# A diagonal block's score tiles computed over part of their columns, the rest read back transposed

## The chip, the cores and the metric

The program runs on one core of one Trainium2 chip. The metric is the device time of one execution in microseconds (us), the median of several runs. Beside the runs there is one profiled execution, whose trace gives every duration below. Engine names are the profile's: PE is TensorE's matmul, PEld its weight load, DVE is VectorE, ACT ScalarE, POOL GpSimd, SP SyncE, which issues the DMAs spoken of here.

## What is computed

Three layers follow each other. The change touches the first alone.

```python
def _attn_ref(u, v, z):              # u, v: 8 x 3072 x 256; z: 8 x 3072 x 64
    scores = (1.0 / S) * np.matmul(z, z.transpose(0, 2, 1))
    attn = np.maximum(scores, 0.0) ** 2
    return u * np.matmul(attn, v)
# x = that, as 24576 rows of 256
# _moe_ref:  h = x @ w_in (256 x 2048);  x = (h * sigmoid(h)) @ w_out
# _moe2_ref: each row goes to the one expert of 8 with the largest logit,
#            gate * sigmoid(...) * (relu(row @ w1[e]) @ w2[e])
```

The scores of a batch are a symmetric matrix: `attn[k, q] == attn[q, k]`.

## The kernel before, in words

All matmuls are in fp32r, in a split form: an operand is stored as a rounded part `hi` and a rest `lo`, and a product takes three passes (hi by hi, lo by hi, hi by lo). Each batch has six blocks of 512 query columns (`q`, `NS` = 4 tiles of 128 each), 48 blocks over the eight batches, written (batch, q) below. A block goes over 24 key tiles of 128 rows (`k`). One key tile is one attention item:

- Its front (lines 257 to 281) makes the 128 x 512 tile `a` of squared scores. Two score passes on PE (lines 269 and 270), Relu and Square on ACT (272 and 273), a copy to `hi` on ACT or DVE (275, 277). One step later DVE takes the rest, `lo = a - hi` (251).
- Its back, three steps (`LOOK`) later, adds the tile to the block's output with six passes of 512 columns (lines 293 to 295).

Because scores are symmetric, a tile whose key block lies below the query block (`mirrored`, from block (0, 3) on) isn't computed. When block `k // NS` computed the transposed tile, `keep` (line 239) stored it to DRAM in a buffer `sym`; `load_sym` (line 225) fetches it in four DMAs that put each 32 x 32 piece in its place, and `flip` (line 232) transposes the pieces on DVE. Such an item has no score passes, one ACT copy (264) and two DVE operations.

The order of the keys in a block is `key_order`: first the four tiles of the next query block, then all others from 0 upwards. So the block's own four tiles, those on the diagonal, stand next to each other, and all four are computed in full.

Between the attention items stand the items of the first MoE layer for the block before. The order is written out by hand (`order`): two MoE items, three attention items, and again, eight times a block. A MoE item has six passes of 512 columns in its front (324), a Sigmoid on ACT (326), a product on DVE (328), `hi` on ACT (331), `lo` on DVE (333), and twelve passes of 256 columns in its back (358 to 360).

Everything else is a task with a release and a due step, taken from a queue: a task that isn't due is run early only when a credit allows it. An item gives credit when its back is done: a MoE item 1.1, a computed attention item 0.8, a mirrored one nothing (`spare`). Most of these tasks are the router's dot products on DVE (line 368), 32 for each block, two to a task of 0.72.

The loads of `z`, `v` and mirrored tiles go through one stream in order of their due steps. Each takes one of four `raw` buffers. A load is put on SP when its turn comes in the stream and its `since` step is past; the loads behind it in the stream wait for it. The operation that uses a load is emitted at its due step, or before if credit allows.

Of the kernel before, what the change touches and what calls it, by code (L numbers as in the profile page):

```python
# [9 lines left out]
F32 = mybir.dt.float32  # L10
# [3 lines left out]
AF = mybir.ActivationFunctionType  # L14
# [3 lines left out]
P = 128  # L18
TQ = 512
NS = TQ // P  # L20
# [3 lines left out]
SQ = 32  # L24
# [9 lines left out]
def r32(ap):  # L34
    return ap.bitcast(F32)
# [7 lines left out]
def moe_chain(tc, zT, uT, vp, win, wout, w12, wgT, wogT, out):  # L43
    nc = tc.nc
    B, NQ, DZ, _ = zT.shape
# [4 lines left out]
    KT = S // P  # L50
# [17 lines left out]
    with ExitStack() as ctx:  # L68
        ec = ctx.enter_context
        dram = ec(tc.tile_pool(name="dram", bufs=1, space=bass.MemoryType.DRAM))  # L70
        cp = ec(tc.tile_pool(name="cp", bufs=1))
# [10 lines left out]
        def mk(pool, shape, dt, tag, bufs):  # L82
            uid[0] += 1
            return pool.tile(shape, dt, tag=tag, name=f"{tag}_{uid[0]}", bufs=bufs)

        def psum():
            return mk(pp, [P, TQ], F32, "ps", 4)

        def accum():
            return mk(pp, [P, 2, TQ], F32, "acc", 2)  # L90
# [58 lines left out]
        def later(steps, cost, fn, slack=2):  # L149
            i = now[0] + steps  # L150
            bisect.insort(queue, (i + slack, i, len(tasks), cost, fn))
            tasks.append(None)
# [32 lines left out]
        def load_u(b, q):  # L185
            t = mk(cp, [P, ND, TQ], F32, "xf", 1)
            x = xs[(b, q)] = [t[:, c, :] for c in range(ND)]
            for c in range(ND):
                nc.sync.dma_start(out=x[c], in_=uT[b, q, :, c, :])
# [19 lines left out]
        def mirrored(b, q, k):  # L209
            return k // NS < q and (b, q) >= (0, 3)  # L210

        def key_order(b, q):
            if not any(mirrored(b, q, k) for k in range(KT)):
                return list(range(KT))
            lead = list(range((q + 1) * NS, (q + 2) * NS)) if q < NQ - 1 else list(range(q * NS, KT))
            return lead + [k for k in range(KT) if k not in lead]

        sym, flipped = {}, {}

        def load_sym(b, q, k):  # L220
            def f(t):
                src = sym[b, k // NS, q]
                for g in range(P // SQ):
                    o = k % NS * P + g * SQ
                    nc.sync.dma_start(out=t[g * SQ:(g + 1) * SQ].rearrange("t (j d) -> t j d", d=SQ),
                                      in_=src[:, o:o + SQ].rearrange("(j t) d -> t j d", t=SQ))
            return f

        def flip(b, q, k):
            def f(t):  # L230
                a = flipped[b, q, k] = mk(cp, [P, TQ], F32, "t1", 4)
                nc.vector.transpose(a, t)  # L232
            return f

        def keep(b, q, k, a):
            key = (b, q, k // NS)
            if key not in sym:
                sym[key] = dram.tile([TQ, TQ], F32, name=f"sym_{b}_{q}_{k // NS}")
            nc.sync.dma_start(out=sym[key][k % NS * P:(k % NS + 1) * P, :], in_=a)

        def att_items(b, q, hold):
            st = {}
            early = (b, q) < (0, 2)
            ks = key_order(b, q)

            def front(i):
                k = ks[i]

                def low(a, hi, lo):
                    def f():  # L250
                        nc.vector.tensor_tensor(out=lo, in0=a, in1=r32(hi), op=ALU.subtract)  # L251
                        if k // NS > q and mirrored(b, k // NS, q * NS):
                            keep(b, q, k, a)
                    return f

                def f():
                    if i == KT - UAT:
                        load_u(b, q)
                    hi = mk(cp, [P, TQ], F32R, "hi", 4)
                    lo = mk(cp, [P, TQ], F32R, "lo", 4)  # L260
                    st[i] = (hi, lo)
                    if mirrored(b, q, k):
                        a = flipped.pop((b, q, k))
                        nc.scalar.activation(hi, a, AF.Copy)  # L264
                        return low(a, hi, lo)
                    h, l = qs[(b, q)]
                    ps = psum()
                    lhs = hl[k // NS][:, (k % NS) * P:(k % NS + 1) * P]
                    nc.tensor.matmul(ps, lhs, h, start=True, stop=False)  # L269
                    nc.tensor.matmul(ps, lhs, l, start=False, stop=True)  # L270
                    a = mk(cp, [P, TQ], F32, "t1", 4)
                    nc.scalar.activation(a, ps, AF.Relu)
                    nc.scalar.activation(a, a, AF.Square)
                    if (early and q and k % 2) or (not early and (q or k % 3)):
                        nc.scalar.activation(hi, a, AF.Copy)  # L275
                    else:
                        nc.vector.tensor_copy(hi, a)
                    return low(a, hi, lo)
                return f

            def back(i):
                k = ks[i]

                def f():
                    hi, lo = st.pop(i)
                    if i == 0:
                        st["acc"] = accum()
                    acc = st["acc"]
                    for c in range(ND):
                        o = k % 2 * D + c * P  # L290
                        h = vh[k // 2][:, o:o + P]
                        l = vl[k // 2][:, o:o + P]
                        nc.tensor.matmul(acc[:, c, :], h, hi, start=i == 0, stop=False)  # L293
                        nc.tensor.matmul(acc[:, c, :], h, lo, start=False, stop=False)  # L294
                        nc.tensor.matmul(acc[:, c, :], l, hi, start=False, stop=i == KT - 1)  # L295
                    if i == KT - 1:
                        later(1, 1.2, finish, 0)
                        later(3, 1.2, lambda: split_x(b, q, hold == "last"), 0)
                return f

            def finish():
                for c, x in enumerate(xs[(b, q)]):
                    nc.vector.scalar_tensor_tensor(out=x, in0=st["acc"][:, c, :], scalar=AS, in1=x, op0=ALU.mult, op1=ALU.mult)

            def spare(k):
                return EARLY if early else 0.0 if mirrored(b, q, k) else 0.8

            return [Item(front(i), back(i), spare(k)) for i, k in enumerate(ks)]
# [399 lines left out]
        for n in range(3, NBLK):  # L708
            for g in range(8):
                if n > 3 or g >= 2:  # L710
                    j = (g - 2) % 8 * GM
# [16 lines left out]
        def att_step(n, k):  # L728
            return at_["a", n, k]
# [12 lines left out]
        def prep(due, rel, load, use, since=0):  # L742
            stream.append((due, rel, len(stream), load, use, since))
# [5 lines left out]
        def last_use(n, keys):  # L749
            direct = [k for k in keys if not mirrored(*blocks[n], k)]  # L750
            return used(n, direct) if direct else 0
# [12 lines left out]
        for n, (b, q) in enumerate(blocks):  # L764
            if q == 0:
                for j in range(NHL):
                    if n:
                        due = att_step(n - 2, KT // 2 + 2 * j) if j < NQ - 2 else att_step(n - 1, KT // 2) if j < NQ - 1 else att_step(n, KT // 2)
                        rel = max(last_use(n - t, range(j * NS, (j + 1) * NS)) for t in range(1, NQ + 1)) + 1
                    else:  # L770
                        due, rel = max(att_step(n, j * NS) - 2, 0), 0
                    prep(due, rel, load_zz(b, j), f_hl(j))
            prep(att_step(n, 0) - (5 if n else 0), att_step(n - 1, KT // 2) if n else 0, load_zz(b, q), f_hh((b, q)))
            for i, k in enumerate(key_order(b, q)):
                if mirrored(b, q, k):
                    o = key_order(b, k // NS)
                    since = max(att_step(n - q + k // NS, o.index(q * NS + s)) for s in range(NS)) + 2
                    prep(att_step(n, i), att_step(n, i), load_sym(b, q, k), flip(b, q, k), since)
            if q == 0:
                for j in range(KT // 2):  # L780
                    rel = used(n - 1, (2 * j, 2 * j + 1)) + LOOK + 1 if n else 0
                    due = att_step(n, 2 * j) + (-1 if n else 1)
                    prep(due, rel, load_flat(vp[b, :, 2 * j:2 * j + 2, :].rearrange("p a d -> p (a d)")), f_split(vh[j], vl[j], b, due))
        stream.sort()
        staged = []
# [84 lines left out]
        for n in range(NBLK):  # L870
            rel = moe_end[n] + LOOK + 2
            due = moe_end[n + 1] if n + 1 < NBLK else max(m2_at[min(NA // 4, 8)], rel)
# [138 lines left out]
```

## Time and profile before

| | us |
|---|---|
| median of 3 runs (lowest and highest) | 5292.82 (5292.71 to 5293.24) |
| the profiled execution | 5293.77 |
| its span, first to last instruction | 5292.0 |
| PE busy | 5189.7 (98%) |
| PE weight load busy | 4529.6 (86%) |
| DVE busy | 3897.6 (74%) |
| ACT busy | 3234.9 (61%) |

A mean of 98% for PE is over stages that differ: blocks (0, 0) to (0, 2), a stage in which attention and MoE items alternate (277.8 to about 4069 us), and the experts. The granted clock is 0.995 of full speed over the span and 1.00 in the middle stage. A matmul's printed duration includes the way through the array, which overlaps the next pass; what a pass costs in a row of passes is the distance between two starts.

### The profile page before, as it was taken

How to read it: one execution, taken by the hardware profiler on the slowest of the kernel's cores; microseconds unless marked ns; L12 is line 12 of the kernel's file. 1: busy time of each engine (PE TensorE's matmuls, PEld its weight loads, DVE VectorE, ACT ScalarE, POOL GpSimd, SP SyncE). 2: the span in 40 equal slices, each digit the busy share in tenths (PEclk: the TensorE clock that was granted, in tenths of full speed). 3: DMA queues.
4: the chain of work that ended last, by engine and by line, in shares of the span. 5: the costliest groups of instructions: out<-in, count | busy, mean ns of one | idle time of the engine just before them, and what ended most of it. 6: DMA issues, size and time to landing. Idle time of an engine off the chain costs nothing.

```text
span 5292.0 us, 88328 instructions
## 1 busy us (share of the span) xinstructions
PE 5189.7 (98%) x30026; PEld 4529.6 (86%) x30026; DVE 3897.6 (74%) x9627; ACT 3234.9 (61%) x5804; POOL 491.2 (9%) x503
## 2 busy tenths in 40 slices
PE   7999999999999999999999999999999899999998
PEld 5888888888888888888888888888888799999998
DVE  8778767866786778677767877687677786666687
ACT  6655665666566666665666566656654455555576
POOL 3100000000000000000000000000000121111111
PEclk9999999999999999999999999999999899999999
DMA  5134324433442334234333432343333456555564
GB/s 155 57 81 86 102 80 92 93 89 77 86 104 85 81 77 110 81 77 84 108 80 82 87 106 75 83 91 95 86 83 80 133 171 201 175 175 175 178 229 157
DMA packets 1334523, 574.63 MB, mean 109 GB/s; under 512 B 1173421, under 2 KB 1206830, under 8 KB 1318192
## 3 DMA queue, kind: packets, MB, share of 16 engines
q1 hardware_dynamic: 1315248, 517.00, 38.1%
q0 software_dynamic: 18816, 51.93, 2.7%
q8 instruction: 237, 3.88, 0.3%
q14 instruction: 222, 1.82, 0.1%
HBM read 393.54 MB, written 178.42 MB: 108 GB/s over the span
## 4 chain that ended last, share of the span: by engine, by line
PE 84%; DVE 8%; ACT 3%; issue 2%; DMA 2%; SPq 0%; POOL 0%; DVEq 0%; ACTq 0%; POOLq 0%
PE ps L324 17%; PE ps L663 10%; PE acc L360 9%; PE acc L358 9%; PE acc L359 9%; PE acc L295 8%; PE acc L294 8%; PE acc L293 8%; PE ps L269 3%; PE ps L270 3%; DVE lo L251 1%; DMA raw<-sym 1%; DVE lo L333 1%; DVE junk L368 1%; DVE t L328 1%
## 5 line engine op out<-in xcount | busy, mean ns | idle before, releaser
L328 DVE TENSOR_TENSOR t<-ps,t 128x512 f32<-128x512 f32 x768 | 529.4, 689 | 655.5 <-ACT t L326 649.8
L359 PE MATMUL acc<-woutl,hi 128*128 128x256 f32 x3600 | 998.3, 277 | 0.0
L331 ACT ACTIVATE hi<-t 128x512 fp32r<-128x512 f32 x768 | 486.0, 633 | 764.1 <-DVE t L328 764.1
L294 PE MATMUL acc<-lo,vh 128*128 128x512 f32 x2304 | 911.1, 395 | 37.7 <-DVE lo L251 37.5
L295 PE MATMUL acc<-hi,vl 128*128 128x512 f32 x2304 | 910.9, 395 | 0.0
L293 PE MATMUL acc<-hi,vh 128*128 128x512 f32 x2304 | 903.3, 392 | 0.0
L360 PE MATMUL acc<-wouth,lo 128*128 128x256 f32 x3072 | 858.5, 279 | 42.5 <-DVE lo L333 42.4
L251 DVE TENSOR_TENSOR lo<-t,hi 128x512 fp32r<-128x512 f32 x1152 | 791.4, 688 | 130.9 <-ACT hi L275 128.9
L358 PE MATMUL acc<-wouth,hi 128*128 128x256 f32 x3072 | 853.9, 278 | 0.0
L359 PEld LDWEIGHTS acc<-woutl,hi 128*128 128x128 f32 x3600 | 678.0, 188 | 32.4
L368 DVE CUSTOM_DVE_ANT_0 junk<-rec,wg 128x256 f32<-128x256 f32 x1536 | 648.7, 422 | 35.3
L360 PEld LDWEIGHTS acc<-wouth,lo 128*128 128x128 f32 x3072 | 577.9, 188 | 53.0 <-DVE lo L333 50.9
L326 ACT ACTIVATE t<-ps 128x512 f32<-128x512 f32 x768 | 454.6, 592 | 265.5 <-PE ps L324 263.7
L358 PEld LDWEIGHTS acc<-wouth,hi 128*128 128x128 f32 x3072 | 577.6, 188 | 26.2
L294 PEld LDWEIGHTS acc<-lo,vh 128*128 128x128 f32 x2304 | 433.9, 188 | 158.3 <-DVE lo L251 56.5
L434 POOL DMA_INDIRECT scr<-rec,si x192 | 206.7, 1077 | 3767.2 <-DVE lo L251 1705.9
L264 ACT ACTIVATE hi<-t 128x512 fp32r<-128x512 f32 x468 | 295.8, 632 | 418.7 <-DVE t L232 333.9
L333 DVE TENSOR_TENSOR lo<-t,hi 128x512 fp32r<-128x512 f32 x768 | 523.6, 682 | 13.1 <-issue 0.2
L293 PEld LDWEIGHTS acc<-hi,vh 128*128 128x128 f32 x2304 | 434.2, 188 | 98.8
L295 PEld LDWEIGHTS acc<-hi,vl 128*128 128x128 f32 x2304 | 434.3, 189 | 91.4
L666 ACT ACTIVATE hi<-ps 128x512 fp32r<-128x512 f32 (+1 forms) x488 | 254.7, 522 | 396.9 <-PE ps L663 375.3
L668 DVE SCALAR_TENSOR_TENSOR lo<-ps,hi 128x512 fp32r<-128x512 f32 (+1 forms) x488 | 288.2, 591 | 245.8 <-ACT hi L666 244.0
(449 smaller groups left out, 10572.9 us busy)
## 6 DMA issues: line engine op xcount, KB each, us to landing
raw<-in_w_dram SPq DMA_DIRECT2D x122, 1024.0 KB
sym<-t SPq DMA_DIRECT2D x468, 256.0 KB
raw<-sym SPq DMA_DIRECT2D x1872, 64.0 KB
raw<-in_zT_dram SPq DMA_DIRECT2D x192, 128.0 KB
raw<-in_vp_dram SPq DMA_DIRECT2D x96, 256.0 KB
xf<-in_uT_dram SPq DMA_DIRECT2D x96, 256.0 KB
xg<-scr SPq DMA_DIRECT2D x39, 544.0 KB
x<-scr SPq DMA_DIRECT2D x304, 64.0 KB
```

Source lines behind the costliest of these rows:

```text
L251: nc.vector.tensor_tensor(out=lo, in0=a, in1=r32(hi), op=ALU.subtract)
L293: nc.tensor.matmul(acc[:, c, :], h, hi, start=i == 0, stop=False)
L294: nc.tensor.matmul(acc[:, c, :], h, lo, start=False, stop=False)
L295: nc.tensor.matmul(acc[:, c, :], l, hi, start=False, stop=i == KT - 1)
L324: nc.tensor.matmul(ps, win_at(w, c, f_), x[c], start=c == 0 and i == 0, stop=c == ND - 1 and i == 2)
L328: nc.vector.tensor_tensor(out=g, in0=ps, in1=sg, op=ALU.mult)
L333: return lambda: nc.vector.tensor_tensor(out=lo, in0=g, in1=r32(hi), op=ALU.subtract)
L358: nc.tensor.matmul(y[:, s, :], a, wh, start=first and s % per_bank == 0, stop=False, skip_group_check=True)
L359: nc.tensor.matmul(y[:, s, :], a, wl, start=False, stop=False, skip_group_check=True)
L360: nc.tensor.matmul(y[:, s, :], l, wh, start=False, stop=last, skip_group_check=True)
L368: nc.vector.tensor_tensor_reduce(out=j, in0=a, in1=w, scale=1.0, scalar=0.0, op0=ALU.mult, op1=ALU.add, accum_out=res)
L663: nc.tensor.matmul(ps[:, 0:T], w[:, o:o + P], y[c][:, 0:T], start=c == 0 and j == 0, stop=c == ND - 1 and j == 2)
```

## The change

From block (0, 3) on, a new function `columns(b, q, k)` says how many of a tile's 512 columns are fetched and not computed: all for a tile below the diagonal, none above it, and on the diagonal 0, 128, 256 and 384 for the block's own tiles 0 to 3 (called own tile 0 to 3 below).

- The two score passes, Relu and Square of an own tile go over the columns from `w` on. The columns before `w` are fetched from `sym` and transposed into the same buffer, by the same `load_sym` and `flip`, cut to `w` columns.
- Own tiles 0 to 2 are stored by `keep`, from the column behind the diagonal piece on (`c`).
- `key_order` spreads the own tiles: they are the block's items 0, 6, 12 and 18. Between them the tiles of the next block come first, then the others. For q = 0 it changes the order too.
- An own tile's `since` is two steps behind the last own tile before it, and `v`'s due steps follow the new order. `spare` isn't changed: an own tile still gives a credit of 0.8.

The core of the diff:

```diff
+        def columns(b, q, k):
+            if (b, q) < (0, 3):
+                return 0
+            return TQ if k // NS < q else k % NS * P if k // NS == q else 0
         def key_order(b, q):
-            if not any(mirrored(b, q, k) for k in range(KT)):
+            if not any(columns(b, q, k) for k in range(KT)):
                 return list(range(KT))
-            lead = list(range((q + 1) * NS, (q + 2) * NS)) if q < NQ - 1 else list(range(q * NS, KT))
-            return lead + [k for k in range(KT) if k not in lead]
+            own = range(q * NS, (q + 1) * NS)
+            lead = [k for k in range(KT) if k // NS == q + 1]
+            o = lead + [k for k in range(KT) if k not in lead and k not in own]
+            for s, k in enumerate(own):
+                o.insert(s * KT // NS, k)
+            return o
...
-                nc.vector.transpose(a, t)
+                w = columns(b, q, k)
+                nc.vector.transpose(a[:, 0:w], t[:, 0:w])
...
+            c = (k % NS + 1) * P if k // NS == q else 0
-            nc.sync.dma_start(out=sym[key][k % NS * P:(k % NS + 1) * P, :], in_=a)
+            nc.sync.dma_start(out=sym[key][k % NS * P:(k % NS + 1) * P, c:TQ], in_=a[:, c:TQ])
...
-                        if k // NS > q and mirrored(b, k // NS, q * NS):
+                        if k // NS > q and mirrored(b, k // NS, q * NS) or k // NS == q and k % NS < NS - 1 and columns(b, q, k + 1):
                             keep(b, q, k, a)
...
-                    nc.tensor.matmul(ps, lhs, h, start=True, stop=False)
-                    nc.tensor.matmul(ps, lhs, l, start=False, stop=True)
-                    a = mk(cp, [P, TQ], F32, "t1", 4)
-                    nc.scalar.activation(a, ps, AF.Relu)
-                    nc.scalar.activation(a, a, AF.Square)
+                    w = columns(b, q, k)
+                    nc.tensor.matmul(ps[:, w:TQ], lhs, h[:, w:TQ], start=True, stop=False)
+                    nc.tensor.matmul(ps[:, w:TQ], lhs, l[:, w:TQ], start=False, stop=True)
+                    a = flipped.pop((b, q, k)) if w else mk(cp, [P, TQ], F32, "t1", 4)
+                    nc.scalar.activation(a[:, w:TQ], ps[:, w:TQ], AF.Relu)
+                    nc.scalar.activation(a[:, w:TQ], a[:, w:TQ], AF.Square)
...
-                if mirrored(b, q, k):
+                if columns(b, q, k):
                     o = key_order(b, k // NS)
-                    since = max(att_step(n - q + k // NS, o.index(q * NS + s)) for s in range(NS)) + 2
+                    since = max(att_step(n - q + k // NS, o.index(q * NS + s)) for s in range(NS if mirrored(b, q, k) else k % NS)) + 2
                     prep(att_step(n, i), att_step(n, i), load_sym(b, q, k), flip(b, q, k), since)
...
-                    due = att_step(n, 2 * j) + (-1 if n else 1)
+                    due = min(att_step(n, key_order(b, q).index(2 * j + s)) for s in range(2)) + (-1 if n else 1)
```

Two places show how this moves instructions. The first is DVE in block (2, 3), from the end of items 6 to 8 to the next attention items. `t` from `ps` is a MoE item's product, `lo` a rest, `junk` with the row behind it one router dot product, STREAM_TRANSPOSE a flip. Before:

```order
L328 TENSOR_TENSOR t_3378_14656<-ps_14647,t_3377_14654 128x512
L251 TENSOR_TENSOR lo_14624<-t_3368_14616,hi_14623 128x512
L328 TENSOR_TENSOR t_3383_14677<-ps_14668,t_3382_14675 128x512
L333 TENSOR_TENSOR lo_14659<-t_3378_14656,hi_14658 128x512
L232 STREAM_TRANSPOSE t_3386_14689<-raw_14499 128x512
```

In the change, the same place:

```order
L342 TENSOR_TENSOR t_3415_14927<-ps_14918,t_3414_14925 128x512
L264 TENSOR_TENSOR lo_14895<-t_3405_14887,hi_14894 128x512
L382 ISA junk_14939,L_14878<-rec_14775,wg 128x256
L382 ISA L_14878 128x1
L382 ISA junk_14941,L_14878<-rec_14775,wg 128x256
L382 ISA L_14878 128x1
L342 TENSOR_TENSOR t_3422_14952<-ps_14943,t_3421_14950 128x512
L347 TENSOR_TENSOR lo_14930<-t_3415_14927,hi_14929 128x512
L244 STREAM_TRANSPOSE t_3425_14964<-raw_14828 128x512
```

Item 6 is own tile 1 here, and its credit of 0.8 lets one more pair of dot products run between the two MoE products. Earlier in the same piece item 6's flip is 128 columns wide, where it was 512.

The second place is SP in block (2, 0), around the first fetched piece of an own tile. `sym_2_0_0` holds the diagonal block of batch 2, `sym_2_0_1` and `sym_2_0_2` the blocks beside it. Before, the loads of `sym` in this block were those for the next block and came behind the store of tile 11; here only `v`, `z` and stores stood:

```order
L179 DMA raw_2652_11552<-in_vp_dram 128x512
L239 DMA sym_2_0_1_11564<-t1_2650_11530 128x512
L179 DMA raw_2658_11582<-in_vp_dram 128x512
L162 DMA raw_2659_11585<-in_zT_dram 64x512
L163 DMA raw_2659_11585<-in_zT_dram 64x512
L239 DMA sym_2_0_1_11564<-t1_2656_11559 128x512
```

In the change:

```order
L252 DMA sym_2_0_2_11776<-t1_2675_11739 128x512
L236 DMA raw_2687_11805<-sym_2_0_0_11603 32x4x32 x4
L179 DMA raw_2689_11812<-in_vp_dram 128x512
L179 DMA raw_2690_11814<-in_vp_dram 128x512
L179 DMA raw_2694_11833<-in_vp_dram 128x512
L162 DMA raw_2695_11835<-in_zT_dram 64x512
L163 DMA raw_2695_11835<-in_zT_dram 64x512
L179 DMA raw_2696_11839<-in_vp_dram 128x512
L252 DMA sym_2_0_0_11603<-t1_2688_11810 128x256
```

Own tile 1's load comes behind the store of item 5, and the loads of `v` that used to run ahead now stand behind it in one run, ahead of own tile 1's store.

## Rows read from the trace of the kernel before

**Rows 1.** Busy time per engine of the middle stage, then of batch 1's six blocks:
```profile
core 0: us, PE busy (x) PEld busy (x) DVE busy (x) ACT busy (x) POOL busy (x), PEclk, DMA share, GB/s
277.80:4069.00 3791.20, 3765.15 (x20619) 3234.37 (x20618) 2794.65 (x6952) 2363.92 (x4018) 197.41 (x222) 1.00 0.37 87
...
522.00:614.30 92.30, 90.27 (x486) 76.44 (x484) 65.29 (x172) 65.56 (x115) 9.27 (x10) 1.00 0.34 111
614.30:700.80 86.50, 86.50 (x476) 74.51 (x475) 57.05 (x146) 60.06 (x102) 4.27 (x5) 1.00 0.30 84
868.60:952.20 83.60, 82.14 (x452) 70.21 (x451) 66.37 (x162) 47.53 (x82) 0.97 (x1) 1.00 0.42 79
952.20:1031.10 78.90, 78.90 (x441) 68.57 (x440) 65.36 (x155) 41.40 (x72) 3.16 (x4) 1.00 0.48 94
```

**Rows 2.** What PE waited for in that stage: us in total, times, longest:
```profile
PE acc L360 <- DVE lo L333: 15.4, 30, 0.9
PE acc L294 <- DVE lo L251: 8.8, 9, 1.1
```

**Rows 3.** Timeline of PE: start us, us, line, operation; the distance of passes by width:
```profile
4142.94 0.28 PE L360 MATMUL acc<-wouth,lo 128*128 128x256 f32 x1
4143.06 0.60 PE L644 MATMUL ps<-ident,xg 128*128 128x128 f32 x4
...
4895.09 0.28 PE L358 MATMUL acc<-b2w,hi 128*128 128x256 f32 x1
...
4896.48 1.54 PE L663 MATMUL ps<-t,b2w 128*128 128x512 f32 x6
4897.85 0.28 PE L358 MATMUL acc<-b2w,hi 128*128 128x256 f32 x1
```

**Rows 4.** One line's instructions: the 128-column transposes, the score pass, flips, loads, stores:
```profile
L644 PE MATMUL ps<-ident,xg x96: 270/272/273, 4143.1 to 5260.9; 128*128 128x128 f32 x96
...
L269 PE MATMUL ps<-hh,hl x684: 391/393/792, 6.8 to 4008.4; 128*128 128x512 f32 x171
...
L232 DVE STREAM_TRANSPOSE t<-raw x468: 698/705/714, 279.6 to 4061.0; 128x512 f32<-128x512 f32 x156
...
L225 SPq DMA_DIRECT2D raw<-sym x1872: 302/487/2055, 100.8 to 4058.7; - x188
L239 SPq DMA_DIRECT2D sym<-t x468: 319/320/1266, 42.4 to 3932.5; - x156
```

**Rows 5.** Groups by line and shape: busy us, mean ns, idle before; ACT by width:
```profile
L273 ACT ACTIVATE t<-t 128x512 f32<-128x512 f32 x684 | 432.7, 633 | 22.3
L666 ACT ACTIVATE hi<-ps 128x512 fp32r<-128x512 f32 x312 | 186.8, 599 | 346.1 <-PE ps L663 335.4 <-issue 8.4 <-ACT rec L691 0.9
L666 ACT ACTIVATE hi<-ps 128x256 fp32r<-128x256 f32 x176 | 67.9, 386 | 50.9 <-PE ps L663 39.8 <-ACT b2w L96 3.0 <-ACT winh L96 2.8
```

**Rows 6.** Timelines of SP, then DVE, at the end of the middle stage: a load's landing:
```profile
4049.71 9.52 SPq L225 DMA_DIRECT2D raw<-sym  x18
...
4061.05 0.71 DVE L232 STREAM_TRANSPOSE t<-raw 128x512 f32<-128x512 f32 x1 [0.47 <-DMA raw<-sym]
```

**Rows 7.** Timelines of DVE, then PE, in block (2, 3): how far `lo` leads its pass:
```profile
1316.66 0.42 DVE L368 CUSTOM_DVE_ANT_0 junk<-rec,wg 128x256 f32<-128x256 f32 x1
...
1317.12 0.42 DVE L368 CUSTOM_DVE_ANT_0 junk<-rec,wg 128x256 f32<-128x256 f32 x1
...
1318.08 0.68 DVE L251 TENSOR_TENSOR lo<-t,hi 128x512 fp32r<-128x512 f32 x1
1319.35 0.69 DVE L328 TENSOR_TENSOR t<-ps,t 128x512 f32<-128x512 f32 x1 [0.58 <-ACT t L326]
1319.95 0.68 DVE L333 TENSOR_TENSOR lo<-t,hi 128x512 fp32r<-128x512 f32 x1
...
1320.89 0.28 PE L360 MATMUL acc<-wouth,lo 128*128 128x256 f32 x1
```

**Rows 8.** What SP's queue waited for: us in total, times, longest:
```profile
SPq L239 <- ACT t L273: 1212.3, 386, 9.0
SPq L225 <- DVE t L232: 788.3, 162, 26.4
```

More of the change, by code (lines that the diff above doesn't have):

```diff
@@ L221, in f @@
             def f(t):
-                src = sym[b, k // NS, q]
+                src, w = sym[b, k // NS, q], columns(b, q, k)
                 for g in range(P // SQ):
                     o = k % NS * P + g * SQ
-                    nc.sync.dma_start(out=t[g * SQ:(g + 1) * SQ].rearrange("t (j d) -> t j d", d=SQ),
-                                      in_=src[:, o:o + SQ].rearrange("(j t) d -> t j d", t=SQ))
+                    nc.sync.dma_start(out=t[g * SQ:(g + 1) * SQ, 0:w].rearrange("t (j d) -> t j d", d=SQ),
+                                      in_=src[0:w, o:o + SQ].rearrange("(j t) d -> t j d", t=SQ))
             return f
```

## The prediction

> **What bounds the kernel now.** I read the busy time by stage first. In the middle stage PE is busy for 3765 of 3791 us, and in blocks 1 and 5 of batch 1 for the whole block [rows 1]. DVE and ACT have room in every block; the tightest is block 5, where DVE works 65.4 of 78.9 us. The reader should see two kinds of block: those where PE never idles, and blocks 0 and 4, where it idles 2.0 and 1.5 us. Next I read what PE waited for: 24 of the stage's 26 idle us are waits for a `lo` from DVE [rows 2]. So the stage is bound by the number and length of PE's passes, with DVE close behind at a few places. All that the change touches lies in this stage, in 45 of the 48 blocks. Last I read the timelines, for what a pass costs by its width [rows 3] and for how far `lo` is ahead of the pass that needs it [rows 7].
>
> **PE's passes.** Six 512-column passes start at 4896.48 and the next pass at 4897.85: 0.228 us each. The twelve 256-column passes ahead of them take 4895.09 to 4896.48: 0.116 us each [rows 3]. Both are proportional to the columns. Per pass, then:
>
> - Own tile 1, 384 columns: on that line 0.171 us, 0.057 less.
> - Own tile 2, 256 columns: 0.116 us, 0.112 less.
> - Own tile 3, 128 columns: no such fp32r pass is in the trace. If proportional it costs 0.058 us and saves 0.170. If the array gains nothing from narrowing it below 256, in the worst case it costs as much as a full pass, 0.228, and saves nothing. The nearest row is the four 128-column transposes by a matmul: 0.60 us in all, of which the last is 0.272 long [rows 3, 4], so (0.60 - 0.27) / 3 = 0.11 us from start to start. That is double the proportional value. They are of another type and mode, but load 128 x 128 weights each like ours, so I take 0.11 and save 0.118.
>
> Each own tile has two score passes. The sum is 2 x (0.057 + 0.112 + 0.118) = 0.574 us a block, times 45 = **25.8 us**. With the bounds of the 128-column pass, 2 x 0.169 x 45 = 15.2 us to 2 x 0.339 x 45 = 30.5 us. The six passes of the item's back are unchanged.
>
> The Trainium skill (TensorE: Matmul & The Clock Gate, Back-to-back issue gap) gives about 81 ns per weight load and matmul at 128 columns in a stream, and 131 ns at 512. The trace's 228 ns at 512 doesn't agree with that page. By its 81 ns the sum would be 28.4 us. The same page (LDWEIGHTS) says that a load takes columns / 1.2 ns whatever the matmul does, 107 ns for 128 columns. That speaks against the narrowest pass; by it the sum would be 26 us, and no fp32r row here shows it.
>
> **ACT.** Relu and Square lose 128 + 256 + 384 = 768 columns a block each. From 512 to 256 columns an ACT instruction goes from 599 to 386 ns, 0.83 ns a column [rows 5], so ACT loses 2 x 0.64 = 1.3 us a block. It is hidden behind PE, so I count nothing, but the chain from scores to `hi` gets shorter.
>
> **DVE.** Three flips a block are added, of 128, 256 and 384 columns. A 512-column flip takes 0.705 us [rows 4]; in proportion that is 1.06 us a block, 48 us in all, and at most 2.1 us a block if width doesn't matter. The cover is DVE's own slack, 13 us in block 5 and more elsewhere [rows 1]. It isn't evenly spread. In block (2, 3) a MoE item's `lo` is done at 1320.63 and its pass starts at 1320.89: 0.26 us [rows 7]. If that cover goes, PE waits in front of that pass.
>
> So I follow the piece of the order that front shows. Own tile 1 is a computed item among mirrored ones, and its credit lets a pair of dot products move up into it: 2 x 0.46 = 0.93 us by the distance of their starts [rows 7]. Against that stand three things. The flip of own tile 1 is 0.18 instead of 0.705 us: 0.53 less. DVE idled 0.58 us just there for a Sigmoid [rows 7], which depends on PE and ACT, so part of the pair falls into a hole. And own tile 1's two score passes give PE 0.34 us of work where a mirrored item had none. 0.93 - 0.53 - 0.34 is 0.06 us, so the lead stays about as it was, before the hole is counted. Where own tiles stood, four in a row, mirrored ones stand now; the number of dot products a block is the same. I take no change of PE's waits: 0, with bounds of 12 us less (half of the 3.5 us of blocks 0 and 4 gone in seven batches, since `v`'s splits no longer run in one train) and 12 us more.
>
> **SP and the DMAs.** Added are 135 x 4 = 540 loads of 0.487 us and 135 stores of 0.320 us [rows 4]: 306 us of issuing over the stage's 3791 us. SP's queue waited 1212 us there for tiles to store and 788 us for `raw` buffers [rows 8], so it has room. The new wait is that an own tile's load needs the store of the one before. Behind it stand loads for tiles several items later, and stores that hold one of four `t1` buffers; the store was issued six items before the load's flip, so it costs nothing.
>
> The places where that can fail can be counted from the stream's rule. A load is put out only when some other use in the stream is emitted. Own tiles 1 and 3 of block 0, and own tile 3 of block 1, have none after their `since`: their load stands at the step of their flip, in batches 1 to 7, **21 places**. But SP isn't tied to DVE's step. Its instruction ahead of such a load is the store of the item before [the second place shown], and two MoE steps lie between, each 12 passes of 0.228 = 2.7 us. Four issues take 1.95 us. At the end of the stage the last load was issued by 4059.23 and its flip started at 4061.05: landed within 1.8 us [rows 6]. The path is 3.8 us, under a cover of 5.5. So I count nothing; the cover gone would cost up to 3.8 us a place.
>
> **The sum.** The profiled execution took 5293.77 us, span 5292.0. 5293.77 - 25.8 = 5268.0. The median is 0.95 us below the profiled execution, so I predict **5267 us**. 0.2% is 10.6 us, about what a measurement of this kernel can tell from no change.
>
> **The rivals.**
>
> - *The 128-column pass gains nothing.* Two narrow passes and the next item's load of 128 x 128 weights could take as long as before. For it: the 128-column transposes are no cheaper than 256-column passes to within 0.01 us [rows 3]. Against: they are no dearer either. Time: 5293.8 - 15.2 = 5279 us.
> - *DVE's pile-up, slower.* Place: items 6, 12 and 18 of a block, where the own tile's credit brings a pair of dot products into a run in which `lo` leads by a quarter of a microsecond. If PE waits out the pair less that lead, 0.93 - 0.26 = 0.67 us at each of 135 tiles, that is 90 us: 5358 us. It decides from (25.8 + 10.6) / 135 = 0.27 us a tile on. For it: the 0.26 us. Against: the reckoning above, and that blocks 0 and 1 leave DVE 27 and 29 us free [rows 1].
> - *Late loads.* The 21 places each hold DVE, then PE. If 1 us of the path shows at each, 5289 us: the gain is mostly given back. For it: in block 0 the loads of `v` queue behind the same load. Against: the cover worked out above.
> - *Idle time is won back as well.* Blocks 0 and 4 lose half of their idle time: 5268 - 12 = 5256 us.
>
> That the change doesn't do what it says is excluded: the built order has the narrow passes and flips.
>
> **How the numbers follow.** Forecast 0.45. Pass without gain 0.22, faster in three quarters of it, since 5 us given back would bring it inside 0.2%. Late loads 0.14, within 0.2%. Pile-up 0.10, slower. Idle won back 0.09. That gives faster 0.45 + 0.17 + 0.09 = 0.70 (rounded), same 0.05 + 0.14 = 0.20 (rounded), slower 0.10. The range reaches from 30.5 us saved with 12 us of idle time won back, 5251, to late loads, 5290; outside is the pile-up and little else.
>
> **What would show it.** In the changed profile: two score passes of 128 columns that start 0.11 us apart (0.06 or 0.23 decides the first rival); each block of the middle stage 0.5 to 0.6 us shorter; PE's waits for `lo` at 24 us, give or take 12; DVE 48 us busier; no wait of DVE for `raw` ahead of the narrow flips. If blocks 3 to 5 grow while PE's busy time falls, the pile-up is right. If DVE waits for a `raw` at own tiles 1 and 3 of block 0, the late loads are. The prediction is wrong if PE's busy time in the middle stage doesn't fall by 15 us at least.

## The result, and the profile after

| | before | changed |
|---|---|---|
| median of the runs (lowest to highest), us | 5292.76 (5291.62 to 5293.24) | 5236.32 (5234.1 to 5237.27) |
| ratio, 95% interval | | 0.9892 (0.9879 to 0.9904) |
| span of the profiled execution | 5292.0 | 5232.3 |

56.4 us less, where 25.8 were forecast. The gain is split by stage first. Busy time by windows, of the kernel before in its last stage, which [rows 1] didn't hold:

```profile
4069.00:5292.00 1223.00, 1184.78 (x8248) 1101.83 (x8246) 881.29 (x2292) 685.46 (x1470) 220.60 (x214) 0.98 0.57 175
```

and of the changed kernel: first stage, middle stage, last stage, then blocks 0, 1, 4 and 5 of batch 1 (length, then PE, PEld, DVE, ACT, POOL; granted clock):

```profile
0.00:277.30 277.30, 241.03 (x1162) 194.54 (x1163) 221.34 (x385) 185.57 (x317) 73.50 (x67) 0.98 0.32 102
277.30:4029.10 3751.80, 3738.65 (x20618) 3220.81 (x20617) 2838.66 (x7099) 2291.03 (x4018) 199.35 (x220) 1.00 0.42 98
4029.10:5232.30 1203.20, 1185.20 (x8248) 1102.16 (x8246) 880.75 (x2280) 684.83 (x1470) 218.03 (x216) 0.99 0.58 178
519.50:608.60 89.10, 88.86 (x483) 75.91 (x482) 63.09 (x161) 63.31 (x114) 4.43 (x6) 1.00 0.37 116
608.60:694.60 86.00, 86.00 (x476) 74.24 (x476) 57.93 (x149) 58.24 (x102) 4.26 (x5) 1.00 0.30 87
861.30:943.20 81.90, 80.97 (x448) 69.25 (x447) 67.80 (x166) 42.11 (x76) 0.00 (x0) 1.00 0.55 104
943.20:1023.20 80.00, 79.61 (x447) 69.16 (x446) 68.57 (x169) 44.03 (x78) 7.81 (x9) 1.00 0.50 103
```

Three things changed:

- PE's busy time in the middle stage fell from 3765.15 to 3738.65, by 26.5 us.
- Its idle time there fell from 26.05 to 13.15 us, by 12.9; blocks 0 went from 92.3 to 89.1 us [rows 1].
- The last stage, in which no instruction was changed, is 19.8 us shorter; PE is as busy there as before.

The sum is 59.2 us, and 59.7 with the first stage: the difference of the spans. (The medians differ by 56.4; of the change's four executions the profiled one is the shortest.) What PE waited for, in the middle stage of the changed kernel (against [rows 2]), then in its last stage:

```profile
PE acc L374 <- DVE lo L347: 6.8, 21, 0.6
PE acc L308 <- DVE lo L264: 4.8, 15, 0.6
...
PE acc L374 <- DVE lo L347: 4.7, 2, 3.7
```

The last stage of the kernel before has this row instead, one wait of 23.8 us:

```profile
PE acc L360 <- DVE lo L333: 24.9, 2, 23.8
```

**The narrow passes.** Timeline of PE in the changed kernel at an own tile 3:

```profile
4011.66 0.28 PE L374 MATMUL acc<-wouth,lo 128*128 128x256 f32 x1
4011.77 0.22 PE L283 MATMUL ps<-hh,hl 128*128 128x128 f32 x1
4011.83 0.28 PE L284 MATMUL ps<-ll,hl 128*128 128x128 f32 x1
4011.94 0.45 PE L307 MATMUL acc<-hi,vh 128*128 128x512 f32 x1
4012.23 0.40 PE L308 MATMUL acc<-lo,vh 128*128 128x512 f32 x1
4012.47 0.40 PE L309 MATMUL acc<-hi,vl 128*128 128x512 f32 x1
```

From start to start the 128-column passes take 0.06 and 0.11 us, and the pass behind them 0.29, 0.06 more than the 0.23 that such a pass takes elsewhere. Over all 45 blocks the medians of a pair are 0.349 us (384 columns), 0.238 (256) and 0.171 (128), and 0.467 for a full pair.

**Flips and ACT.** Groups by line and shape in the changed kernel (busy us, mean ns), the narrow flips and the Square of own tiles:

```profile
L244 DVE STREAM_TRANSPOSE t<-raw 128x384 f32<-128x384 f32 x45 | 25.7, 572 | 0.0
L244 DVE STREAM_TRANSPOSE t<-raw 128x256 f32<-128x256 f32 x45 | 19.8, 439 | 0.0
L244 DVE STREAM_TRANSPOSE t<-raw 128x128 f32<-128x128 f32 x45 | 13.7, 304 | 0.0
...
L287 ACT ACTIVATE t<-t 128x384 f32<-128x384 f32 x45 | 23.7, 526 | 1.4
L287 ACT ACTIVATE t<-t 128x256 f32<-128x256 f32 x45 | 18.9, 419 | 1.4
L287 ACT ACTIVATE t<-t 128x128 f32<-128x128 f32 x45 | 14.0, 311 | 1.4
```

None of the 135 narrow flips waited for its load: the idle time in front of them, the last number, is 0.0. Over the middle stage DVE is busy for 44.0 us more than before (2794.65 to 2838.66).

**The seam of the stages.** When a block's dot products are done, a task `pick` chooses each row's expert on DVE, and four steps later a task `rank` scatters the block's rows to a buffer `scr` in DRAM, by four indirect DMAs on POOL (line 434, 448 in the change). The last stage's tiles are gathered from `scr` by DMAs on SP. For block (7, 3), block 45 of all, the kernel before has `pick` at step 1901 of the program and `rank` at 1905, behind the first two gathers of that same step. In the change the last dot products fall earlier: `pick` is at step 1899 and `rank` at 1903, ahead of the gathers. In brackets stands how long the engine was idle before an instruction, and what ended that. Timelines of DVE (first instruction of `pick`), POOL (first scatter) and ACT (copy into a `rec` buffer that the scatters must have left) in the kernel before:

```profile
4079.57 0.18 DVE L401 TENSOR_REDUCE m<-L 128x4 f32<-128x32 f32 x1
...
4108.45 0.99 POOL L434 DMA_INDIRECT scr<-rec,si  x1 [96.47 <-DMA xg<-scr]
...
4119.67 1.09 ACT L350 ACTIVATE rec<-acc 128x512 f32<-128x512 f32 x2 [26.18 <-DMA scr<-rec,si]
```

and in the changed kernel:

```profile
4032.82 0.18 DVE L415 TENSOR_REDUCE m<-L 128x4 f32<-128x32 f32 x1
...
4047.56 1.17 POOL L448 DMA_INDIRECT scr<-rec,si  x1 [82.20 <-DVE t L342]
...
4059.99 1.08 ACT L364 ACTIVATE rec<-acc 128x512 f32<-128x512 f32 x2 [7.21 <-DMA scr<-rec,si]
```

Before, the scatters waited for the gathers. From `pick` to ACT's copy it took 40.1 us, of which ACT waited 26.2; now 27.2, of which it waited 7.2. Behind that copy on ACT stand the Sigmoids of the last MoE block, so DVE and PE wait too.

### The profile page after: what moved, and what is told of

Read it like the earlier page. It is cut to its first block, busy times and chain, and to the rows that moved or that the text cites. A ratio compares the mean times of both kernels' runs of the same rounds, so it can differ in the third digit from the quotient of the medians.

```text
span 5232.3 us, 90181 instructions
## 1 busy us (share of the span) xinstructions
PE 5164.9 (99%) x30026; PEld 4517.5 (86%) x30026; DVE 3940.7 (75%) x9762; ACT 3161.4 (60%) x5804; POOL 490.9 (9%) x503
## 4 chain that ended last, share of the span: by engine, by line
PE 82%; DVE 9%; issue 3%; DMA 2%; ACT 2%; SPq 1%; POOL 0%; DVEq 0%; ACTq 0%; POOLq 0%
PE ps L338 16%; PE ps L677 10%; PE acc L374 9%; PE acc L372 9%; PE acc L373 9%; PE acc L308 8%; PE acc L309 8%; PE acc L307 8%; PE ps L284 2%; PE ps L283 2%; DVE junk L382 2%; DVE lo L264 2%; DMA raw<-sym 2%; SPq L236 1%; DVE lo L347 1%
```

## The experiments

The theories: **A**, the gain is 27 us of passes, 13 of PE's waits and 20 at the seam, the last two by order alone; **B**, the extra gain comes from the narrow tiles; **C**, the order pays in the middle stage only. D and E came later. Each run was timed beside the kernel before, whose median was 5293.93 us for the first four runs and the last two, 5294.43 for the next four, 5295.49 for the ninth and tenth. Ratios are to these.

**1. The order alone.**

```diff
-            return TQ if k // NS < q else k % NS * P if k // NS == q else 0
+            return TQ if k // NS < q else 0
```

(`key_order` is left as in the change.)

> The changed kernel's order of key tiles, with own tiles computed in full: no narrow passes, no flips, loads or stores for own tiles. Theory A (three parts: 27 us from shorter score passes, 13 us from waits of PE that the new order takes out of the middle stage, 20 us from one wait at the start of the last stage, which the order also takes out): 5293 - 13 - 20 = 5260 us, PE busy in the middle stage as before at 3765 us, idle there 13 instead of 26 us. Theory B (the extra gain comes from the narrow tiles themselves, through shorter chains and a less loaded ACT): 5293 us, idle as before. Theory C (the order pays in the middle stage alone, the last stage's wait follows from how early DVE and ACT get there): 5280 us.

5278.80 us, ratio 0.9970 (0.9959 to 0.9982). Windows of this run: middle stage, last stage, block 0 of batch 1.

```profile
278.71:4074.28 3795.57, 3768.43 (x20620) 3237.69 (x20619) 2808.18 (x6965) 2350.01 (x4018) 194.01 (x220) 1.00 0.37 87
4074.28:5278.70 1204.42, 1185.63 (x8247) 1102.10 (x8245) 878.70 (x2280) 685.22 (x1470) 221.24 (x216) 0.99 0.58 178
522.00:613.70 91.70, 89.78 (x484) 76.28 (x483) 62.55 (x159) 65.06 (x114) 4.49 (x6) 1.00 0.32 105
```

A is right about the seam: the last stage is short, so that gain is the order's. It is wrong about the middle stage, where PE idles 27.1 us, as before: the order doesn't remove those waits. There B is right so far. C is wrong on both stages; that its 5280 us were nearly met is luck. The middle stage is even 4.4 us longer than before, 1.1 of it idle time and 3.3 PE's busy time (run 4 below shows what lengthens that).

**2 and 3. The seam, from both sides.** In the kernel before, `rank` of block 45 one step earlier:

```diff
-                later(4, 0.6, rank)
+                later(3 if n == NSNAP - 1 else 4, 0.6, rank)
```

> The kernel before with one number changed: the rank step of block 45 comes three steps after its pick instead of four, so that its four scatters stand ahead of the first two gathers of the last stage instead of behind them. Theory A: the wait of 23.8 us of PE for a lo at the start of the last stage goes down to about 4 us, 5273 us, the middle stage unchanged. Theory C (the wait is set by when the work ahead is done, not by scatter against gather): 5293 us; the gathers then wait for the scatters and PE as long as before.

and in the change two steps later:

```diff
-                later(4, 0.6, rank)
+                later(6 if n == NSNAP - 1 else 4, 0.6, rank)
```

> The changed kernel with the reverse: the rank step of block 45 six steps after its pick, so that its scatters stand behind the first two gathers. Theory A: the long wait comes back, 5236 + 20 = 5256 us, middle stage unchanged. Theory C: 5236 us, since the work ahead is done as early as in the changed kernel.

The first took 5280.77 us, ratio 0.9974 (0.9964 to 0.9984), the second 5247.12, ratio 0.9910 (0.9895 to 0.9925). Their middle stages are 3790.1 and 3752.1 us, as in the kernel each is made from; the difference is at the seam, but it is 13 us of the 20: the last stages take 1210.3 and 1216.0 us, where the two kernels have 1223.0 and 1203.2. The second scatter and ACT's copy in the first run, then the copy in the second (`pick` began at 4077.43 and 4033.45):

```profile
4096.73 0.97 POOL L434 DMA_INDIRECT scr<-rec,si  x1 [6.50 <-DMA scr<-rec,si]
4105.20 1.09 ACT L350 ACTIVATE rec<-acc 128x512 f32<-128x512 f32 x2 [13.88 <-DMA scr<-rec,si]
...
4072.38 1.08 ACT L364 ACTIVATE rec<-acc 128x512 f32<-128x512 f32 x2 [18.96 <-DMA scr<-rec,si]
```

With the two kernels of the last section this makes a table of two by two. The chain from `pick` to the copy takes 40.1 and 38.9 us with the gathers first, 27.8 and 27.2 with the scatters first: 12 us by that order. What ACT has to do meanwhile is 13.9 us where `pick` stands at step 1901, 20.0 where it stands at 1899: 6 us by the earlier pick. Together 18 of the 20 us. Theory A holds for the seam, but with two causes: the order of the transfers, and how early the block's dot products are done.

**4. Block 0 of each batch as before**, the rest as changed:

```diff
-            if (b, q) < (0, 3):
+            if (b, q) < (0, 3) or q == 0:
```

> The changed kernel with block 0 of each batch as before: natural order of its key tiles, own tiles in full. Seven blocks lose 0.6 us of shorter passes each, 4 us. Theory A1 (the 12 us of waits of PE that blocks 0 lost were lost by their new order, which spreads the v splits and own tiles): 5236 + 4 + 12 = 5252 us, blocks 0 of about 92 us again. Theory A2 (they were lost by what the other blocks' order leaves over to block 0): 5240 us, blocks 0 of about 90 us.

5257.18 us, ratio 0.9930 (0.9916 to 0.9943), 21 us above the change and 5 above A1. The waits of blocks 0 are back. Windows of this run around one of them, and the pass that waited:

```profile
529.00:531.00 2.00, 0.23 (x2) 0.03 (x1) 1.05 (x3) 1.94 (x5) 0.00 (x0) 1.00 0.69 239
531.00:534.50 3.50, 3.47 (x13) 3.20 (x14) 3.50 (x6) 3.40 (x7) 0.00 (x0) 0.52 0.35 98
...
531.03 0.48 PE L374 MATMUL acc<-wouth,lo 128*128 128x256 f32 x1 [1.80 <-DVE lo L347]
```

PE, busy for 8.88 of the 9.0 us before, waits 1.80 us for a `lo`, and then the granted clock is 0.52, the level of 1.2 GHz: passes of 512 columns start 0.43 us apart. Such a wait can cost more than its length. It needn't: each of the seven blocks 0 of this run has one wait of 1.7 to 2.2 us, and behind four of them the granted clock fell to 0.50 for a while; in run 1 the waits are 1.6 to 2.4 us, and it fell behind three of seven. (In the kernel before, the waits in these blocks are shorter, 0.9 us at most (`lo` of line 333, [rows 2]), and it fell behind none.) What decides is not shown. With run 1 it follows that neither the order nor narrow tiles in the other blocks remove these waits; block 0 needs both, or something that comes with both.

**What comes with both.** The stream hands each load's release step on to all behind it (`r_ = max(r_, rel)`). An own tile's load has the step of its flip as release. So the twelve splits of `v` at a batch's start, which the kernel before takes up as fast as credit allows, wait in the change for the own tiles between them. Timelines of DVE grouped by tile, eleven splits of batch 1 with first and last start, in the kernel before and in the change:

```profile
L94 DVE TENSOR_TENSOR vl<-raw,vh x11: 678/684/686, 518.3 to 546.6; 128x512 fp32r<-128x512 f32 x11
...
L94 DVE TENSOR_TENSOR vl<-raw,vh x11: 680/686/693, 514.0 to 584.5; 128x512 fp32r<-128x512 f32 x11
```

28 us became 71. Each split takes 0.6 us of ACT and 0.7 of DVE ahead of some `hi` or `lo`. This is **theory D**; **E** is that narrow tiles shorten the work there.

**5 and 6. Spreading the splits in the kernel before**, without and with an earlier `rank`:

```diff
-                    rel = used(n - 1, (2 * j, 2 * j + 1)) + LOOK + 1 if n else 0
                     due = att_step(n, 2 * j) + (-1 if n else 1)
+                    rel = max(used(n - 1, (2 * j, 2 * j + 1)) + LOOK + 1, due - 6) if n else 0
```

> The kernel before, with one rule changed: a v split may come at most six steps ahead of the step at which it is due, so that the twelve splits at a batch's start are spread over block 0 and do not come in a train in its first ten steps. No narrow pass, no flip, the key order as before. Theory D (in the changed kernel the loads for own tiles do this by the stream's running maximum of release steps, and that alone takes the waits out of block 0): the seven blocks 0 lose 1.8 us of idle time each, 5294 - 12 = 5282 us, the last stage as before at 1223 us. Theory E (the waits go because narrow tiles shorten ACT's Relu and Square there): no change, 5294 us.

> The kernel before with the v splits spread as in the run beside it and the rank step of block 45 two steps after its pick instead of four, without any narrow pass. Theory D with A: 12 us less in the middle stage, and at the start of the last stage the chain from pick to the landed scatters takes 28 us less two steps of 2.7 us, against 14 us of cover, so PE waits some 8 instead of 24.9 us: 5294 - 12 - 17 = 5265 us. Theory E: 5277 us.

5283.61 us, ratio 0.9980 (0.9971 to 0.9989), and 5265.81, ratio 0.9946 (0.9933 to 0.9960). The middle stage is 3782.7 us, 8.5 less than before, idle 20.1. That is two thirds of D's 12 us; two waits a block 0 are left, of 0.60 and 0.71 us in batch 1, the first behind two splits on DVE. With the earlier `rank` the last stage takes 1204.6 us. So 29 us, half of the change's gain, are to be had without a narrow pass.

**9. The order with the change's release steps**, own tiles in full (run 1 with an addition):

```diff
+        holds = [att_step(n, key_order(b, q).index(q * NS + s)) for n, (b, q) in enumerate(blocks) if n >= 3 for s in range(1, NS)]
...
-            r_ = max(r_, rel)
+            r_ = max([r_, rel] + [h for h in holds if (h, h) < (due, rel) or h < due])
```

> The changed kernel's key order, own tiles in full, without their loads, flips and stores (as in the first run), but with the release steps that those loads would have put into the stream's running maximum, so that the v splits stand at the very steps of the changed kernel. Theory D: blocks 0 take 89.2 + 0.6 = 89.8 us, the idle time of the middle stage goes from 27 to 14 us, 5279 - 13 = 5266 us. Theory E (narrow tiles are needed for it too): blocks 0 of 91 us or more, 5275 us or more.

5262.74 us, ratio 0.9940 (0.9927 to 0.9954). Windows: middle stage, and block 0 of batch 1.

```profile
277.50:4056.20 3778.70, 3764.68 (x20620) 3236.02 (x20619) 2809.35 (x6964) 2343.92 (x4018) 193.36 (x220) 1.00 0.37 88
...
520.90:610.80 89.90, 89.73 (x484) 76.30 (x483) 62.29 (x159) 64.51 (x114) 4.52 (x6) 1.00 0.37 113
```

Against run 1 nothing but release steps changed. The eleven splits, which started within 24 us there (516.5 to 540.3), take 72 here (515.4 to 587.0), block 0 of batch 1 goes from 91.7 to 89.9 us, the stage's idle time from 27.1 to 14.0. Theory D is right; E isn't needed.

**10. Full passes in the changed kernel**, ACT's narrow operations, flips, loads and stores kept:

```diff
-                    nc.tensor.matmul(ps[:, w:TQ], lhs, h[:, w:TQ], start=True, stop=False)
-                    nc.tensor.matmul(ps[:, w:TQ], lhs, l[:, w:TQ], start=False, stop=True)
+                    nc.tensor.matmul(ps, lhs, h, start=True, stop=False)
+                    nc.tensor.matmul(ps, lhs, l, start=False, stop=True)
```

> The changed kernel, but the two score passes of an own tile run over all 512 columns; Relu, Square, loads, flips, stores and the order are those of the changed kernel. The passes alone: in the changed kernel's trace a pair of full passes takes 0.46 us from start to start and the narrow pairs 0.349, 0.238 and 0.170 us, so 0.62 us a block and 45 x 0.62 = 28 us: 5236 + 28 = 5264 us, waits of PE in the middle stage and at the start of the last one as in the changed kernel. If narrow passes also paid by shorter chains, PE's waits grow too: above 5270 us. If the longer passes fill PE's waits: 5255 us.

5252.47 us, ratio 0.9919 (0.9905 to 0.9932): below all that was expected. The middle stage, and what PE waited for in it:

```profile
277.50:4045.80 3768.30, 3761.29 (x20620) 3232.97 (x20620) 2841.80 (x7100) 2294.80 (x4018) 198.12 (x220) 1.00 0.41 98
...
PE acc L374 <- DVE lo L347: 5.0, 19, 0.4
...
PE acc L308 <- DVE lo L264: 0.3, 1, 0.3
```

What DVE's `lo` of the attention items waited for on ACT, in the middle stage of run 9, then of this run:

```profile
DVE lo L264 <- ACT hi L289: 189.8, 274, 1.5
...
DVE lo L264 <- ACT hi L289: 142.2, 219, 1.1
```

So from run 9 to this one, 10 us are gained with no pass shortened: ACT is busy for 49 us less in the stage (2343.9 to 2294.8), DVE for 32 us more, and PE idles 7.0 instead of 14.0 us. (The other 3.4 us leave PE's busy time, though no pass is shorter: passes are printed 0.39 us long where they start 0.23 apart, so a short wait shows as busy.) The gain should be ACT's, since all else in this step adds work. The traces bear that out: in both runs PE, ACT and DVE do the same operations in the same order but for the flips, and `lo` waits 48 us less for ACT's `hi`. ACT's part alone wasn't tried. With full passes, then, theory B has a share. From here to the change the passes take away 22.6 us of PE's busy time and give back 6.1 us of idle time: the shorter passes wait again for `lo`. Both steps together, run 9 to the change, shorten the middle stage by 26.9 us. The passes alone should give 26.2 (next section), so in the change some 0.7 us is left of ACT's gain, and that is all of theory B's extra gain.

**7 and 8. Better versions.** `rank` of block 45 two steps behind its `pick` (`later(2, 0.6, rank, 0)`, 1901 instead of 1903); then also block (0, 2) mirrored ((0, 2) for (0, 3) in `mirrored` and `columns`):

> The changed kernel with the rank step of block 45 two steps after its pick instead of four: 5.4 us earlier. Theory A (PE's wait there is the chain from pick to the landed scatters less its cover): the 4.7 us that PE still waits at the start of the last stage are gone, 5236 - 4 = 5232 us. If the weight loads of the last stage hold up the scatters instead: 5236 us.

> The changed kernel with the rank step as in the run beside it, and with block 2 of the first batch also mirrored: its eight tiles of the blocks above come by load and flip, its own tiles are narrow. PE loses 8 x 2 passes of 0.23 us and 0.6 us of narrow passes, 4.3 us, in a block where it is busy for 136.6 of 140.7 us; DVE gains 8 flips of 0.7 us. If PE bounds that block: 5232 - 4 = 5228 us. If DVE does, which decodes the weights there: 5232 us or some us more.

5233.65 us, ratio 0.9885 (0.9870 to 0.9900), and 5231.63, ratio 0.9880 (0.9865 to 0.9895). The second is the lowest time measured, with all four runs below all four of the change's, but the ratios' intervals overlap. In run 7 ACT's wait at the seam is 4.5 us instead of 7.2, and PE's 3.8 instead of 4.7, though `rank` came two steps earlier. Most of the rest went to the second scatter, which waited 5.60 us for the first, 1.73 in the change:

```profile
4051.10 0.97 POOL L448 DMA_INDIRECT scr<-rec,si  x1 [5.60 <-DMA scr<-rec,si]
```

The first had started at 4044.34, just behind loads of the last stage's weights (on SP from 4042.60). The first stage of run 8 is only 3.0 us shorter than run 7's, and 1.0 than the change's, so of the 4.3 us little is safe.

**11 and 12. Less credit for own tiles**, run 8 with this line, 0.4 and then 0.0:

```diff
-                return EARLY if early else 0.0 if mirrored(b, q, k) else 0.8
+                return EARLY if early else 0.0 if mirrored(b, q, k) else 0.4 if columns(b, q, k) else 0.8
```

> The version with block 2 mirrored and the earlier rank step, with the credit of a narrow own tile at 0.4 instead of 0.8, so that fewer dot products stand beside it on DVE. If the waits left in blocks 4 and 5 (0.9 and 0.4 us a block) come from dot products there: idle time of the middle stage from 13 to about 8 us, 5231.6 - 5 = 5227 us, with pick and rank of block 45 one step later, 1 to 2 us given back: 5228 us. If they come from flips and splits: 5232 us.

> The same with no credit for a narrow own tile, as for a mirrored one. Pick of block 45 then comes two steps later than in the changed kernel, and its rank two steps after it, so the chain to the landed scatters ends where it did in the changed kernel: some 4.7 us of wait there. If dot products cause the waits in the middle stage: 5228 us; if they only move to other places: 5233 us or more.

5239.10 us, ratio 0.9898 (0.9881 to 0.9914), and 5243.50, ratio 0.9905 (0.9889 to 0.9922): slower by 7 and 12 us than run 8. What PE waited for in the middle stage of each:

```profile
PE acc L308 <- DVE lo L264: 12.3, 15, 0.9
PE acc L374 <- DVE lo L347: 3.4, 16, 0.2
...
PE acc L374 <- DVE lo L347: 10.7, 22, 1.4
PE acc L308 <- DVE lo L264: 9.9, 15, 1.2
```

The dot products move to other places, and the waits with them. In blocks 0, 4 and 5 (means of batches 1 to 7) PE idles 0.3, 0.8 and 0.4 us in run 8, 0.9, 1.2 and 0.1 in run 11, and 1.2, 0.3 and 1.3 in run 12. Where a credit falls decides such waits, and less credit isn't better.

**The steps in a row.** From the kernel before to run 1, to run 9, to run 10 and to the change it is one step each. The medians, with what each step gains (the kernel before itself ran at 5292.8 to 5295.5 us beside them, so a step is known to some 3 us; runs 9 and 10 were timed together):

| | us | gain | where |
|---|---|---|---|
| kernel before | 5292.8 | | |
| + order (run 1) | 5278.8 | 14.0 | seam 18.6, middle stage 4.4 lost |
| + release steps (run 9) | 5262.7 | 16.1 | `v` splits in blocks 0 |
| + flips, loads, stores, narrow ACT (run 10) | 5252.5 | 10.2 | PE's waits for `lo` |
| + narrow passes (change) | 5236.3 | 16.2 | PE's busy time, less waits that return |

## Why the prediction was wrong

The sign was right, and the term that the forecast took for the whole gain was right as well. The time lies 14.7 us below the range, by terms that it put at nothing. What the narrow tiles bring by themselves, from run 9 to the change, is 26.4 us by the medians: the forecast's 25.8. The rest, 30 us, comes from the order and the release steps.

- **PE's passes: right.** The pairs come to 0.349 + 0.238 + 0.171 us, and 0.06 on the pass behind the narrowest. 3 x 0.467 - 0.818 is 0.583 us a block against 0.574, 26.2 us against 25.8; block 1 fell by 0.5 us. PE's busy time fell by 26.5, but that it agrees so closely is partly luck, since short waits count in it: from run 10 to the change, where only passes get shorter, it fell by 22.6. The 128-column pass was put at 0.11 us each; it is 0.06 and 0.11, and the rest of the price stands on the next pass. The rival by which it gains nothing is wrong. The Trainium skill (TensorE: Matmul & The Clock Gate, Back-to-back issue gap) has 81 ns at 128 columns; half a pair here, 85 ns, is near it, but the 60 ns on the pass behind aren't in that. Its 131 ns at 512 is far from the 233 measured.
- **ACT: the size right, the conclusion only in the sum.** Square is 107, 214 and 322 ns shorter at the three widths, Relu as much, 1.3 us a block. "It is hidden behind PE, so I count nothing" doesn't hold with full passes: the step from run 9 to run 10 gains 10 us. In the change, where the shorter passes give it back, nothing was the right count.
- **DVE: about right.** The flips come to 59 us instead of 48, since a narrow one costs more than its share: 0.304 us at 128 columns, 0.705 at 512 [rows 4]. DVE's busy time rose by 44.0. What the flips alone cost PE wasn't tried.
- **PE's waits: the step that failed in the middle stage.** "I take no change of PE's waits: 0" is wrong. PE's idle time fell by 12.9 us, just beyond the bound of 12 and for the reason behind that bound: the splits no longer run in one train. The rival of idle time won back had the mechanism and 0.09 of the chance. Run 9 shows that it is the release steps of the own tiles' loads that break up the train, run 1 that the new key order alone doesn't. Reading it from the stream's rule was possible: the prediction used the release of a load only to ask whether the load comes late, not what it holds back behind it.
- **SP and late loads: right; of the pile-up a little came.** No narrow flip waited. Block 4 of batch 1 has 0.9 us of idle time instead of 1.5, block 5 0.4 instead of none, and block 5 is 1.1 us longer, though each block was to be shorter by 0.5 to 0.6. A part of that is a shift: two more pairs of score passes start in block 5's stretch, two fewer in block 4's. But the two blocks together are only 0.6 us shorter (162.5 to 161.9), where the passes take away 1.2. So some 0.6 us is lost there, over six narrow tiles, where the rival had 0.67 a tile.
- **The stage: the step that failed most.** "All that the change touches lies in this stage" is wrong. The wait of 23.8 us stood in the last stage of the trace of before, and it hung on the step of one task of the first layer's order. The prediction read PE's waits in the middle stage alone. The last stage became 19.8 us shorter, of the 30.6 us that are missing.

## What to carry to other kernels

Read the longest single waits of the whole span before the sum is closed, the joints between stages above all: a change of order can shift a task past a transfer there, and nothing in the changed stage shows it. Where a queue passes a release on to what stands behind, ask of every new entry what it delays, since a delay can also break up a train. And a gain that comes with a change need not be the change's: half of this one is to be had in the old kernel by two small edits (run 6).

## What the runs showed of the hardware

A pair of 128-column passes moves part of its price to the next pass: 0.058 us from start to start for the first, 0.112 for the second and 0.291 instead of 0.231 for the 512-column pass behind. So the pair costs 0.23 us with that, hardly less than one of 256 columns (0.24), behind which the next pass takes 0.236. And a wait of PE of 1.80 us was followed by a granted clock of 0.52 over the next 3.5 us (run 4), while a wait of the same length in run 1, at 532.9 us, was not: there the clock stayed at 1.00. The first of four scatters, issued while the last stage's weights were loading, held up the second for 6.50 us in run 2 and for 5.60 in run 7, against 1.7 to 2.3 us in most cases.
